# Attention, expert layer and cosine layer on one core: the beginning rebuilt

## The chip, the cores and the metric

The kernel runs on one core of a Trainium2 chip. The metric is the device time of one execution in microseconds. Engines are named as in the profile: PE (matrix multiply; PEld its weight loads), DVE (vector), ACT (scalar), POOL (GpSimd) and SP, which only issues DMAs.

## The reference

A decaying linear attention (batch 4, 8 heads, 768 steps, head width 48) feeds two layers over 3072 tokens of width 384:

```python
for t in range(S):
    cur = einsum('bhd,bhe->bhde', u * kt, vt)
    y[:, :, t] = einsum('bhd,bhde->bhe', rt, state + cur)
    state = w * state + einsum('bhd,bhe->bhde', kt, vt)
x = y in token order, heads side by side            # 3072 x 384
p = domain_probs / (domain_probs.sum(-1) + 1e-9)
out = sum over 4 experts e:  p[:, e] * (relu(x @ w1[e]) @ w2[e])   # inner width 1024
h = out @ w_in                                       # inner width 2048
result = (h * cos(h)) @ w_out
```

## The kernel before

**Layers.** The work on PE is a list of items numbered n. An item is one block of 128 inner columns of a unit (an expert part or a part of the cosine layer) for one tile of tokens: `m_up` multiplies into one of two PSUM tiles `hp` (`ups2[n % 2]`), ACT makes `gh` of it and DVE `gl` (`m_relu`; each float32 value is carried as a high and a low part, three products for one), and `m_down`, two or three items later, multiplies these into three accumulators. A layer block is eight items. The first eight items are plain float32 on 256 tokens, with the raw weight blocks `raw_w` (loaded by `raw_load`) and the raw attention result `x_raw`; from n=8 on the weights come through `w_load` (DMA) and `w_split` (ACT the high part, DVE or POOL the low one), eight tiles ahead of their use.

**Attention.** A cell c is 128 time steps of one batch row in two chunks of 64 (24 cells; the first four are the first time block of each batch row). Within a chunk the sum over steps is a masked product of scores (`a_score_pe`, line 191, then the mask in lines 325 and 330 on DVE) with the values; between chunks a state is carried (`a_state_pe`, line 177). A cell needs, beforehand, its loads (`a_load_tok`, `a_load_t`), `a_kt` and `a_ru` on POOL, `a_r`, `a_rk`, `a_kp` and `a_sum` on DVE. `ONE_AT[c]` is the item in which `a_one(c)` puts the cell's scores, state and the output of cell c-1 on PE; `steps_of` gives the items in which the rest is issued. Cells 4 to 8 stand four items apart, the later ones three.

**The beginning.** The first two cells go ahead of item 0, with steps of their own: `powers` (table of powers of w on DVE), `b_r`, `b_ru`, `b_score`, `b_off`, `b_mask`, `b_in`, `b_y` and `b_x`, which ends in `x_raw`. `tails`, `table` and `table2` make the key table `wk_ch`, which all `a_kp` need; `b_states` makes the first states, and stands with cell 2 at n=2. `warm` keeps PE busy from the start on zeros.

**Order.** Every engine executes its instructions in the order in which the program issues them (`tc.manual_schedule`). What an item issues ahead of its matmuls (raw loads, `w_loads`, `w_splits`, the x splits of n=4 to 6) comes first; `mix` then sets the steps of the item between its matmuls; `later` holds what is to be issued some items on. A wait on ACT or DVE therefore holds whatever was issued behind it. In the code of the first eight items:

```python
if n < BLK - 3: raw_load(n + 3, nc.scalar)
if 2 <= n < BLK:
    w_loads(n - 1)
    w_splits(n - 3, nc.gpsimd if n % 2 else None)
if 4 <= n < 4 + KD: split(xh[0][:, n - 4, ...], xl[0][...], x_raw[:, n - 4, :])
```

Of the kernel before, what the change touches and what calls it, by code (L numbers as in the profile page):

```python
# [7 lines left out]
F32 = mybir.dt.float32  # L8
# [18 lines left out]
def attention_moe_cos_mlp_kernel(  # L27
# [97 lines left out]
    def a_load_t(c):  # L125
        b, i = cells[c]
        t = ld_p.tile([128, 2, HP, 128], F32, tag="rkt", name="rkt", bufs=4)
        (nc.scalar if N_FIRST < c < 6 else nc.sync).dma_start(out=t, in_=rkt[b, i])
        ld.setdefault(c, {})["t"] = t
# [5 lines left out]
    def a_load_tok(c):  # L135
        b, i = cells[c]
        (nc.scalar if N_FIRST < c < 6 else nc.sync).dma_start(out=tok_tile(c).rearrange("q x p d -> q (x p d)"), in_=tok_ch[b, i])
# [5 lines left out]
    def a_r(c):  # L143
        t = ld[c]["t"][:, 0]
        nc.vector.tensor_tensor(out=t, in0=t, in1=pw[:, :, 0:128], op=ALU.mult)
# [9 lines left out]
    def a_rk(c):  # L155
        t = ld[c]["tok"]
        nc.vector.tensor_tensor(out=t[:, 0:2], in0=t[:, 0:2], in1=t[:, 2:4], op=ALU.mult)
# [72 lines left out]
    def b_off(c):  # L230
        so = part_of(2 * c, HP * 4 * C, HP * C).rearrange("q (p t) -> q p t", t=C)
        nc.scalar.activation(out=so, in_=ld[c]["off"].rearrange("q (p t) -> q p t", t=C), func=ACTF.Copy)
        ld[c]["so"] = so

    def b_mask(c):
        s_ = t_p.tile([128, 2, HP, C], F32, tag="s", name="s")
        by = ld[c]["ps"].rearrange("q c (p a t) -> q a c p t", p=HP, a=2)
        wide = [128, 2, HP, C]
        nc.vector.tensor_tensor(out=s_, in0=by[:, 0], in1=mask.unsqueeze(1).unsqueeze(1).to_broadcast(wide), op=ALU.mult)
        nc.vector.copy_predicated(  # L240
            out=s_, mask=eye.bitcast(I32).unsqueeze(1).unsqueeze(1).to_broadcast(wide), data=by[:, 1],
        )
        ld[c]["s"] = s_

    def b_in(c, ps):
        d = ld[c]
        tok, s_, so = d["tok"], d["s"], d["so"]
        d["ps_y"] = ps
        for p in range(HP):
            for ch in range(2):  # L250
                for par in range(2):
                    x0, a0 = 64 * (ch ^ par), 64 * ch
                    nc.tensor.matmul(
                        ps[a0:a0 + 64, par, p * D:p * D + D], s_[x0:x0 + 64, ch, p, :], tok[x0:x0 + 64, 4 + ch, p, :],
                        start=p == 0, stop=ch == 0, skip_group_check=True,
                    )
            for par in range(2):
                x0 = 64 * (1 ^ par)
                nc.tensor.matmul(
                    ps[64:128, par, p * D:p * D + D], so[x0:x0 + 64, p, :], tok[x0:x0 + 64, 3, p, :],  # L260
                    start=False, stop=True, skip_group_check=True,
                )

    def b_y(c):
        yo = t_p.tile([128, DM], F32, tag="yo", name="yo", bufs=2)
        ld[c]["yo"] = yo
        nc.scalar.activation(
            out=yo.rearrange("q (p a d) -> q a p d", a=2, d=D),
            in_=ld[c]["ps_y"].rearrange("q a (p d) -> q a p d", d=D), func=ACTF.Copy,
        )  # L270

    def b_x(c, px):
        for kk in range(KD):
            nc.tensor.transpose(px[:, kk * 128:kk * 128 + 128], ld[c]["yo"][:, kk * 128:kk * 128 + 128], ident)
        nc.scalar.activation(
            out=x_raw[:, :, c * 128:c * 128 + 128], in_=px[:, 0:DM].rearrange("q (k t) -> q k t", k=KD), func=ACTF.Copy
        )

    def b_states():
# [133 lines left out]
    def x_in(i, j, lag, cols=slice(0, TB), step=None):  # L413
        src = acc[j].rearrange("q b d -> q (b d)").rearrange("q (k t) -> q k t", k=KD)
        nc.sync.dma_start(out=src[:, :, cols], in_=yd[i].rearrange("(k q) t -> q k t", k=KD)[:, :, cols])
        x_split(src, j, lag, cols, step or X_STEP)
# [8 lines left out]
    def a_x(c):  # L425
        b, i = cells[c]
        if b == B - 1 and i == 0:
            x_in(0, 0, X0_LAG, slice(256, 512), (0, 0, 0))
        if b == B - 1 and i == 1:
            x_in(1, 1, XT_LAG)  # L430
        ld.pop(c)

    NC_ = len(cells)
# [7 lines left out]

    on_pe = (a_one,)
    ONE_AT = {c: 4 * c - 6 for c in range(N_FIRST, 9)}
    ONE_AT.update({c: 29 + 3 * (c - 9) for c in range(9, NC_ + 1)})
    BEGIN = {3: ((a_load_tok, 0), (a_load_t, 0), (a_ru, 1)), 4: ((a_load_tok, 3), (a_load_t, 4), (a_ru, 5)), 5: ((a_load_tok, 6), (a_load_t, 7), (a_ru, 8))}

    def steps_of(c):
        at, p = ONE_AT[c], ONE_AT[c - 1]
        wide = at - p > 3
        two = ONE_AT.get(c - 2, 0)  # L450
        yield from BEGIN.get(c, ((a_load_tok, two - 1), (a_load_t, two), (a_ru, p - (2 if wide else 1))))
        yield from ((a_kt, p), (a_r, p + wide), (a_rk, p + 2), (a_kp, p + 2), (a_sum, p + 2 + wide))

    steps = {}
    for c in range(N_FIRST, NC_ + 1):
# [40 lines left out]
    def raw_load(q, eng=None):  # L496
        (eng or nc.sync).dma_start(out=raw_w[0, 0, q], in_=moe_wb[q])
# [219 lines left out]
    x2_tile = {}  # L717
    x2d = {}

    wu_a = const.tile([128, 128], mybir.dt.bfloat16, name="wu_a")  # L720
    wu_b = const.tile([128, 512], mybir.dt.bfloat16, name="wu_b")

    def warm(n):
        if n == 0:
# [53 lines left out]
            double(n)  # L778
            n *= 2

    def tails():
        for a in range(2):
            x = slice(64 * a, 64 * a + 64)
            for ch in range(2):
                last = 2 * C - 1 - C * (ch ^ a)
                nc.scalar.activation(out=tk[x, :, ch], in_=pw[x, :, last:last - C if last >= C else None:-1], func=ACTF.Copy)

    def table():
        pt = ps_d.tile([128, TB], F32, tag="up", name="pt").rearrange("q (p a e) -> q a p e", p=HP, a=2)
        for p in range(HP):  # L790
            nc.tensor.transpose(pt[:, :, p, :], tk[:, p].rearrange("q c t -> q (c t)"), ident)
        return pt

    def table2(pt, a):
        x = slice(64 * a, 64 * a + 64)
        nc.scalar.activation(out=wk_ch[x], in_=pt[x, ::-1 if a else 1, :, 0:D], func=ACTF.Copy)
# [8 lines left out]
    def prob_load():  # L805
        nc.sync.dma_start(out=p_in, in_=moe_domain_probs.rearrange("(p t) e -> p t e", t=32))
# [48 lines left out]
    N_DEC = N_ATT + 4  # L855
    X_STEP = (0, 0, 1)
    X_LAG = 1
    XT_LAG = 2
    TAIL = 2
    Y_LAG = 1  # L860
    WARM_FIRST = 17
    X0_LAG = 2

    def on_pe_call(f):
# [18 lines left out]

    with tc.manual_schedule():
        nc.vector.memset(wu_a, 0.0)
        nc.scalar.activation(out=uw1, in_=wu_a[:, 0:2 * HP].bitcast(F32), func=ACTF.Copy)
        nc.vector.memset(wu_b, 0.0)
        setup()
        warm(WARM_FIRST)
        powers()  # L890
        raw_load(0)
        a_load_tok(2)
        a_load_t(2)
        nc.sync.dma_start(out=uu_ch.rearrange("q a p d -> q (a p d)"), in_=u_ch)
        for c in range(N_FIRST):
            b_load(c, 3, 5, 1)
        raw_load(1)
        prob_load()
        raw_load(2)
        for c in range(N_FIRST):  # L900
            b_r(c)
            a_kt(c, nc.vector)
        nc.vector.tensor_tensor(out=w128, in0=pw[:, :, 2 * C:2 * C + 1], in1=pw[:, :, 2 * C:2 * C + 1], op=ALU.mult)
        for c in range(N_FIRST):
            b_ru(c)
        off = x_bank()
        b_score(0, pair_ps, off[:, 0:HP * C])
        b_off(0)
        tails()
        b_mask(0)  # L910
        b_score(1, dense_ps[0], off[:, HP * C:2 * HP * C])
        b_off(1)
        b_mask(1)
        a_ru(2)
        a_kt(2)
        b_in(0, dense_ps[1][:, :, 0:HD])
        b_y(0)
        pt = table()
        table2(pt, 0)
        table2(pt, 1)  # L920
        b_in(1, pair_ps[:, :, 0:HD])
        b_y(1)
        b_x(0, dense_ps[0][:, 0])
        b_x(1, dense_ps[0][:, 1])
        a_r(2)
        a_rk(2)
        a_sum(2)
        for c in range(N_FIRST + 1):
            a_kp(c)
        ps_d_ctx.close()  # L930
        ps_u = ctx.enter_context(tc.tile_pool(name="ps_u", bufs=1, space=bass.MemoryType.PSUM))
        ups2 += [ps_u.tile([128, TB], F32, name=f"hp{x}") for x in range(2)]
        for hp in ups2:
            nc.tensor.matmul(hp[:, 256:512], wu_a, wu_b[:, 0:256], start=True, stop=True)
        ps_a = ctx.enter_context(tc.tile_pool(name="ps_a", bufs=1, space=bass.MemoryType.PSUM))
        downs = []
        pend = []
# [1 line left out]
        for n in range(NI + 4):  # L939
            live = n < NI  # L940
            moe2 = False
            if n < BLK - 3:
                raw_load(n + 3, nc.scalar)
            if 2 <= n < BLK:
                w_loads(n - 1)
                w_splits(n - 3, nc.gpsimd if n % 2 else None)
            if n == 3:
                prob_norm()
                prob_scale()
                prob_store()  # L950
# [287 lines left out]
```

## Time and profile before

| | |
|---|---|
| median of 3 runs | 1261.89 us (1261.34 to 1262.25) |
| profiled execution | 1262.03 us, its span 1260.3 us |
| PE busy | 1246.5 us, 99% of the span |
| DVE, ACT, POOL busy | 773.0, 492.9, 193.6 us |
| DMA | 126.53 MB, mean 100 GB/s |

The span is from the first to the last instruction of the program; the rest of the execution's time lies around it. In the timeline a row is a run of like instructions: start, duration, engine, line, operation, out<-in, count, and in brackets the idle time before it with what ended it. "q" behind an engine is its sequencer, which issues DMAs.

### The profile page before, as it was taken

The page shows a single profiled execution, that of the slowest core. Times are in us where ns is not written, and L with a number is a line of the kernel's source. Part 1 is how long each engine was busy: PE and PEld are TensorE (multiplying, and loading weights), DVE is VectorE, ACT ScalarE, POOL GpSimd, SP SyncE. Part 2 cuts the span into 40 slices and gives each one's busy share as a digit, 9 for nine tenths or more (in the row PEclk, how much of TensorE's full clock was granted, in tenths as well). Part 3 has the DMA queues.
Part 4 walks back from the last instruction along what each step waited for, and adds up shares of the span by engine and source line. Part 5 has one row for each costly group of instructions (what it writes and reads, how often), then busy time and mean ns, then how long its engine had stood idle before and what let it go on. Part 6 is the DMA issues. An engine that isn't in the chain of part 4 may idle for free.

```text
span 1260.3 us, 20498 instructions
## 1 busy us (share of the span) xinstructions
PE 1246.5 (99%) x8453; PEld 1038.8 (82%) x8453; DVE 773.0 (61%) x1259; ACT 492.9 (39%) x879; POOL 193.6 (15%) x190
## 2 busy tenths in 40 slices
PE   9999999999999999999999999999999999999997
PEld 7898888788888888888888888888888888888886
DVE  6897747766264464546645543326776777777665
ACT  4442313223221131112111222216777677767774
POOL 3664323421100000111111111112000100010100
PEclk9999999999999999999999999999999999999999
DMA  8635634444242243223331410123001400160601
GB/s 322 220 117 177 196 125 154 124 137 111 84 139 59 84 134 109 67 76 127 107 92 52 133 43 9 59 78 122 1 1 42 160 26 25 36 203 13 196 11 47
DMA packets 72501, 126.53 MB, mean 100 GB/s; under 512 B 23153, under 2 KB 44754, under 8 KB 72402
## 3 DMA queue, kind: packets, MB, share of 16 engines
q1 hardware_dynamic: 65634, 93.38, 23.6%
q0 software_dynamic: 4608, 25.17, 6.4%
q10 hardware_dynamic: 2160, 6.62, 1.5%
q8 instruction: 67, 1.10, 0.4%
q14 instruction: 32, 0.26, 0.1%
HBM read 101.90 MB, written 23.25 MB: 99 GB/s over the span
## 4 chain that ended last, share of the span: by engine, by line


## 5 line engine op out<-in xcount | busy, mean ns | idle before, releaser
L595 PE MATMUL hp<-xh,w 128*128 128x512 f32 (+1 forms) x888 | 341.3, 384 | 1.6 <-DVE gl L609 1.6
L596 PE MATMUL hp<-xl,w 128*128 128x512 f32 (+1 forms) x888 | 338.1, 381 | 0.5 <-DVE xl L118 0.5
L597 PE MATMUL hp<-xh,w 128*128 128x512 f32 (+1 forms) x888 | 337.9, 380 | 0.2 <-issue 0.2
L670 PE MATMUL a<-gh,w 128*128 128x512 f32 (+1 forms) x880 | 335.0, 381 | 0.0
L671 PE MATMUL a<-gh,w 128*128 128x512 f32 (+1 forms) x880 | 334.8, 380 | 0.0
L672 PE MATMUL a<-gl,w 128*128 128x512 f32 (+1 forms) x880 | 334.7, 380 | 0.0
L608 ACT ACTIVATE gh<-hp 128x512 fp32r<-128x512 f32 (+1 forms) x200 | 114.5, 573 | 539.7 <-PE hp L597 532.6
L609 DVE SCALAR_TENSOR_TENSOR gl<-hp,gh 128x512 fp32r<-128x512 f32 (+1 forms) x200 | 131.1, 657 | 299.5 <-ACT gh L608 298.8
L595 PEld LDWEIGHTS hp<-xh,w 128*128 128x128 f32 x888 | 166.9, 188 | 35.7 <-DVE gl L609 2.9
L597 PEld LDWEIGHTS hp<-xh,w 128*128 128x128 f32 x888 | 166.9, 188 | 32.1
L596 PEld LDWEIGHTS hp<-xl,w 128*128 128x128 f32 x888 | 167.0, 188 | 31.9 <-DVE xl L118 0.7
L670 PEld LDWEIGHTS a<-gh,w 128*128 128x128 f32 x880 | 165.5, 188 | 32.0 <-ACT rr L626 0.4
L672 PEld LDWEIGHTS a<-gl,w 128*128 128x128 f32 x880 | 165.5, 188 | 31.7
L671 PEld LDWEIGHTS a<-gh,w 128*128 128x128 f32 x880 | 165.5, 188 | 31.5
L693 POOL TENSOR_TENSOR acc<-acc,pm 128x512 f32<-128x512 f32 (+1 forms) x57 | 72.5, 1302 | 537.9 <-DVE pm L692 537.9
L628 DVE SCALAR_TENSOR_TENSOR hs<-rr,hs 128x512 f32<-128x512 f32 x96 | 67.4, 702 | 62.8 <-ACT rr L627 62.8
L626 ACT ACTIVATE rr<-rr 128x512 f32<-128x512 f32 x96 | 60.8, 633 | 86.4 <-DVE rr L621 86.4
L620 DVE SCALAR_TENSOR_TENSOR rr<-ni,hs 128x512 f32<-128x512 int32 x96 | 66.3, 691 | 45.6 <-ACT ni L619 45.6
L621 DVE SCALAR_TENSOR_TENSOR rr<-ni,rr 128x512 f32<-128x512 int32 x96 | 66.5, 692 | 3.3
L507 POOL DMA_DIRECT2D w<-dec_all x32 | 17.1, 535 | 333.0 <-PE a L672 332.1
L118 DVE TENSOR_TENSOR gl<-hs,gh 128x512 fp32r<-128x512 f32 x96 | 66.0, 688 | 0.7 <-ACT gh L117 0.7
L618 ACT ACTIVATE hs<-hp 128x512 f32<-128x512 f32 x96 | 57.2, 596 | 17.8 <-PE hp L597 17.6
(151 smaller groups left out, 1066.2 us busy)
## 6 DMA issues: line engine op xcount, KB each, us to landing
w<-dec_all POOLq DMA_DIRECT2D x32, 768.0 KB, 4.6
s<-in_moe_wb_dram SPq DMA_DIRECT2D x53, 384.0 KB, 4.0
draw<-in_moe_wb_dram SPq DMA_DIRECT2D x32, 384.0 KB, 4.3
dec_all<-dout SPq DMA_DIRECT2D x32, 384.0 KB, 3.0
tok<-in_tok_ch_dram SPq DMA_DIRECT2D x19, 576.0 KB, 5.4
rkt<-in_rkt_dram SPq DMA_DIRECT2D x21, 512.0 KB, 3.8
pb<-pn SPq DMA_DIRECT2D x24, 256.0 KB, 5.0
out_dram<-acc SPq DMA_DIRECT2D x17, 256.0 KB, 2.5
```

Source lines behind the costliest of these rows:

```text
L595: nc.tensor.matmul(hp, wh[:, kk, :], x_h[:, kk, :], start=kk == 0, stop=False)
L596: nc.tensor.matmul(hp, wh[:, kk, :], x_l[:, kk, :], start=False, stop=False)
L597: nc.tensor.matmul(hp, wl[:, kk, :], x_h[:, kk, :], start=False, stop=kk == KD - 1)
L608: nc.scalar.activation(out=gh, in_=hp, func=ACTF.Relu)
L609: nc.vector.scalar_tensor_tensor(out=gl, in0=hp, scalar=0.0, in1=gh.bitcast(F32), op0=ALU.max, op1=ALU.subtract)
L620: nc.vector.scalar_tensor_tensor(out=rr, in0=ni, scalar=-PI2_HI, in1=hs, op0=ALU.mult, op1=ALU.add)
L621: nc.vector.scalar_tensor_tensor(out=rr, in0=ni, scalar=-PI2_LO, in1=rr, op0=ALU.mult, op1=ALU.add)
L628: nc.vector.scalar_tensor_tensor(out=hs, in0=rr, scalar=1.0, in1=hs, op0=ALU.subtract, op1=ALU.mult)
L670: nc.tensor.matmul(a, wh[:, ds], gh, start=q == 0, stop=False)
L671: nc.tensor.matmul(a, wl[:, ds], gh, start=False, stop=False)
L672: nc.tensor.matmul(a, wh[:, ds], gl, start=False, stop=q == BLK - 1)
L693: nc.gpsimd.tensor_tensor(out=o, in0=o, in1=m, op=ALU.add)
```

## The change

Warming uses three float32 matmuls on zeros in `acc` where 17 bf16 ones stood. The masks and the products with the values of the first two cells go in halves of two heads (`h`), `b_y` and the transposes in parts; the copy into `x_raw` moves from ACT to DVE. `tails` is split, its first half ahead of `b_ru`; `b_off` of both cells comes behind both scores. The key table and the three `a_kp` move to n=1, `b_states` and cell 2 from n=2 to n=3. Loads on SP are reordered, and one more raw block is on SP; the raw and staged weight loads on ACT, and cell 3's loads, come an item later; the splits stay. The two dummy matmuls that filled the upper half of `hp` become two copies on ACT. `a_rk` comes an item earlier for cells three items apart, `a_kp` an item later for cells four items apart; the x splits of the first two token tiles are spread.

```diff
-    def b_mask(c):
+    def b_mask(c, h):
+        if h == 0:
+            ld[c]["s"] = t_p.tile([128, HP, 2, C], F32, tag="s", name="s")
+        heads = slice(2 * h, 2 * h + 2)
...
-    def b_in(c, ps):
+    def b_in(c, ps, h):
...
-        for p in range(HP):
+        for p in range(2 * h, 2 * h + 2):
...
-    def b_x(c, px):
-        for kk in range(KD):
+    def b_x(c, px, k0, k1):
+        for kk in range(k0, k1):
             nc.tensor.transpose(px[:, kk * 128:kk * 128 + 128], ld[c]["yo"][:, kk * 128:kk * 128 + 128], ident)
-        nc.scalar.activation(
-            out=x_raw[:, :, c * 128:c * 128 + 128], in_=px[:, 0:DM].rearrange("q (k t) -> q k t", k=KD), func=ACTF.Copy
+
+    def b_xc(c, px, k0, k1):
+        nc.vector.tensor_copy(
+            out=x_raw[:, k0:k1, c * 128:c * 128 + 128],
+            in_=px[:, k0 * 128:k1 * 128].rearrange("q (k t) -> q k t", t=128),
         )
...
-            x_in(0, 0, X0_LAG, slice(256, 512), (0, 0, 0))
+            x_in(0, 0, X0_LAG, slice(256, 512), (0, 0, 1))
         if b == B - 1 and i == 1:
-            x_in(1, 1, XT_LAG)
+            x_in(1, 1, XT_LAG, step=(0, 1, 2))
...
     ONE_AT = {c: 4 * c - 6 for c in range(N_FIRST, 9)}
+    ONE_AT[N_FIRST] = 3
...
-    BEGIN = {3: ((a_load_tok, 0), (a_load_t, 0), (a_ru, 1)), ...
+    BEGIN = {3: ((a_load_tok, 1), (a_load_t, 1), (a_ru, 2)), ...
...
-        yield from ((a_kt, p), (a_r, p + wide), (a_rk, p + 2), (a_kp, p + 2), (a_sum, p + 2 + wide))
+        yield from ((a_kt, p), (a_r, p + wide), (a_rk, p + 1 + wide), (a_kp, p + 2 + wide), (a_sum, p + 2 + wide))
...
-    wu_a = const.tile([128, 128], mybir.dt.bfloat16, name="wu_a")
-    wu_b = const.tile([128, 512], mybir.dt.bfloat16, name="wu_b")
+    wu_a = part_of(0, 1280, 128)
+    wu_b = part_of(1, 512, 512)
...
-        pt = ps_d.tile([128, TB], F32, tag="up", name="pt").rearrange("q (p a e) -> q a p e", p=HP, a=2)
+        pt = x_bank().rearrange("q (p a e) -> q a p e", p=HP, a=2)
...
-    XT_LAG = 2
+    XT_LAG = 1
-    WARM_FIRST = 17
+    WARM_FIRST = 3
...
         raw_load(0)
-        a_load_tok(2)
-        a_load_t(2)
-        nc.sync.dma_start(out=uu_ch.rearrange("q a p d -> q (a p d)"), in_=u_ch)
         for c in range(N_FIRST):
             b_load(c, 3, 5, 1)
         raw_load(1)
+        a_load_t(2)
+        raw_load(2)
+        a_load_tok(2)
+        nc.sync.dma_start(out=uu_ch.rearrange("q a p d -> q (a p d)"), in_=u_ch)
+        raw_load(3)
         prob_load()
-        raw_load(2)
...
+        tails(0)
         for c in range(N_FIRST):
             b_ru(c)
         off = x_bank()
         b_score(0, pair_ps, off[:, 0:HP * C])
-        b_off(0)
-        tails()
-        b_mask(0)
         b_score(1, dense_ps[0], off[:, HP * C:2 * HP * C])
-        b_off(1)
-        b_mask(1)
+        for c in range(N_FIRST):
+            b_off(c)
+        tails(1)
+        for c in range(N_FIRST):
+            for h in range(2):
+                b_mask(c, h)
         a_ru(2)
         a_kt(2)
-        b_in(0, dense_ps[1][:, :, 0:HD])
-        b_y(0)
-        pt = table()
-        table2(pt, 0)
-        table2(pt, 1)
-        b_in(1, pair_ps[:, :, 0:HD])
-        b_y(1)
-        b_x(0, dense_ps[0][:, 0])
-        b_x(1, dense_ps[0][:, 1])
+        b_in(0, dense_ps[1][:, :, 0:HD], 0)
+        b_in(0, dense_ps[1][:, :, 0:HD], 1)
+        b_y(0, 0, HP)
+        b_in(1, pair_ps[:, :, 0:HD], 0)
+        b_y(1, 0, 2)
+        px = (x_bank(), dense_ps[1][:, 0])
+        b_x(0, px[0], 0, KD)
+        b_xc(0, px[0], 0, KD)
+        b_in(1, pair_ps[:, :, 0:HD], 1)
+        b_x(1, px[1], 0, 1)
+        b_xc(1, px[1], 0, 1)
+        b_y(1, 2, HP)
+        b_x(1, px[1], 1, KD)
+        b_xc(1, px[1], 1, KD)
         a_r(2)
...
-        for c in range(N_FIRST + 1):
-            a_kp(c)
...
-        for hp in ups2:
-            nc.tensor.matmul(hp[:, 256:512], wu_a, wu_b[:, 0:256], start=True, stop=True)
...
-            if n < BLK - 3:
-                raw_load(n + 3, nc.scalar)
-            if 2 <= n < BLK:
-                w_loads(n - 1)
+            if n < 2:
+                nc.scalar.activation(out=ups2[1 - n][:, 256:512], in_=wu_b[:, 0:256], func=ACTF.Copy)
+            if 2 <= n < BLK - 2:
+                raw_load(n + 2, nc.scalar)
+            if 3 <= n < BLK:
+                w_loads(n - 2)
                 w_splits(n - 3, nc.gpsimd if n % 2 else None)
-            if n == 3:
+            if n == 1:
+                pt = table()
+                for a in range(2):
+                    table2(pt, a)
+                for c in range(N_FIRST + 1):
+                    a_kp(c)
+            if n == 4:
                 prob_norm()
```

## Rows read from the trace of the kernel before

**Rows 1.** Stages: stretch, length, engines' busy (count), PE clock, DMA share, GB/s.

```profile
15.17:37.19 22.02, 22.02 (x327) 19.18 (x325) 15.74 (x27) 9.59 (x22) 10.43 (x11) 1.00 0.90 308
37.19:110.00 72.81, 69.99 (x1314) 66.72 (x1313) 62.78 (x97) 26.98 (x62) 44.92 (x36) 1.00 0.56 180
```

**Rows 2.** PE's waits from 18 to 110 us: total, times, longest.

```profile
PE hp L595 <- DVE gl L609: 1.4, 2, 1.1
PE hp L357 <- DVE gl L609: 0.7, 1, 0.7
PE hp L596 <- DVE xl L118: 0.5, 1, 0.5
```

**Rows 3.** PE's waits from 150 to 400 us.

```profile
PE pair_ps L177 <- DVE kp L166: 0.9, 1, 0.9
PE hp L357 <- DVE gl L609: 0.4, 1, 0.4
```

**Rows 4.** Timeline of the beginning: start, duration, engine, line, operation, count, idle before.

```profile
1.34 5.80 PE L728 MATMUL hp<-wu_b,wu_a 128*128 128x512 bf16 x17 [1.34 <-DVE wu_b L887]
...
5.14 0.15 PEld L728 LDWEIGHTS <-wu_a 128*128 128x128 bf16 x1 [0.27 <-issue]
...
5.47 1.18 PEld L728 LDWEIGHTS <-wu_a 128*128 128x128 bf16 x6 [0.18 <-issue]
...
6.07 2.45 ACT L206 ACTIVATE acc<-acc,uw 128x128 f32<-128x128 f32 x8 [3.74 <-DVE acc L199]
...
8.97 1.44 ACT L786 ACTIVATE acc<-pw 64x256 f32<-64x256 f32 x4
...
9.36 0.63 PE L225 MATMUL px<-acc,rkt 64*64 64x64 f32 x16
...
10.98 0.66 PE L791 MATMUL pt<-ident,acc 128*128 128x128 f32 x4
11.10 0.49 ACT L267 ACTIVATE yo<-dy_ps 128x384 f32<-128x384 f32 x1 [0.27 <-PE dy_ps L259]
...
12.65 0.55 PE L274 MATMUL ds_ps<-ident,yo 128*128 128x128 f32 x3
...
15.17 2.75 PE L589 MATMUL hp<-acc,raw_xh 128*128 128x256 f32 x12
```

**Rows 5.** What line 325 waited for in the whole run: total us, times.

```profile
  PE pair_ps L177: 21.1, 14
```

**Rows 6.** Timeline of ACT and its DMA issues, 14 to 28 us.

```profile
14.84 0.44 ACTq L137 DMA_DIRECT2D tok<-in_tok_ch_dram  x1
...
22.64 0.44 ACTq L137 DMA_DIRECT2D tok<-in_tok_ch_dram  x1
...
27.77 0.84 ACT L504 ACTIVATE w<-s 128x768 fp32r<-128x768 f32 x1 [0.89 <-DMA s<-in_moe_wb_dram]
```

**Rows 7.** DMA issue at 22.64 us: KB, us from issue to landing.

```profile
tok<-in_tok_ch_dram ACTq DMA_DIRECT2D x1, 576.0 KB, 6.5
```

**Rows 8.** Timeline of DVE, POOL and PE, 27.5 to 33 us.

```profile
27.62 0.55 DVE L166 TENSOR_TENSOR kp<-tok,wk_ch 128x384 f32<-128x384 f32 x1
28.96 1.83 DVE L118 TENSOR_TENSOR xl<-acc,xh 128x256 fp32r<-128x256 f32 x1 [0.80 <-ACT xh L117]
...
30.46 1.19 POOL L153 TENSOR_TENSOR tok<-tok,uu_ch 128x384 f32<-128x384 f32 x1
...
31.16 0.54 PE L177 MATMUL pair_ps<-tok,kp 64*48 64x48 f32 x32
```

**Rows 9.** Timeline of DVE, 50 to 55 us.

```profile
51.56 2.19 DVE L166 TENSOR_TENSOR kp<-tok,wk_ch 128x384 f32<-128x384 f32 x1
53.67 0.41 DVE L609 SCALAR_TENSOR_TENSOR gl<-hp,gh 128x256 fp32r<-128x256 f32 x1
```

**Rows 10.** Timeline of DVE, 58 to 63 us.

```profile
59.47 2.58 DVE L118 TENSOR_TENSOR xl<-acc,xh 128x256 fp32r<-128x256 f32 x2
```

**Rows 11.** Timeline of DVE, 231 to 239 us.

```profile
233.40 1.64 DVE L157 TENSOR_TENSOR tok<-tok 128x384 f32<-128x384 f32 x1
```

## The prediction: what the rebuilt beginning does to the time

> **What bounds the kernel now.** I read the busy shares by stage first, then what PE waited for, then the timeline of the beginning. Layer work starts at 15.17 us. From there to 37.19 PE is busy without a break (22.02 of 22.02) while the DMA engines stand at 0.90; from 37.19 to 110 PE misses 2.8 us (69.99 of 72.81), with DVE busy for 62.78 [rows 1]. So a gain can only come from a layer stream that starts earlier, or from the few waits of PE after that. These are, from 18 to 110 us, 1.4 and 0.7 us for gl and 0.5 for xl [rows 2], later 0.9 us for kp and 0.4 for gl [rows 3]: about 4 us in all. What stands at 0.90 of its capacity when the stream begins is the DMA, and this decides whether an earlier start is kept.
>
> **The change, part by part.** Numbers n are layer blocks (items), c attention cells; score(0) is b_score of cell 0.
>
> *Warming.* The 17 bf16 matmuls of 128x512 begin at 1.34. The weight load at 5.14 stands 0.42 us (0.15 busy, 0.27 idle) from the one before; from 5.47 six fit into 1.18 us [rows 4]. 512 columns in 0.42 us is the 1.2 GHz level, in 0.2 us the 2.4 GHz one: PE had run back to back for about 4.1 us when the clock rose, and the warming ends near 7.0. The new warming is 3 float32 matmuls. Six of 128x256 (12 records of line 589) take the 2.6 us from 15.17 [rows 4], 0.43 each at the high level; 128x512 is 0.86 there and 1.72 at the low one, three are 2.6 to 5.2 us. Their memsets are twice as wide, so they start at about 1.7 and, with a rise after the same 4.1 us, end near 6.2. Score(0) then goes with the scaled parts that ACT makes, 0.3 us apart from 6.07 (eight in 2.45), the fourth done at 7.35 [rows 4], and not behind the warming: 0.3 us earlier.
>
> *Off blocks and tails.* The first two tails move into ACT's empty time before 6.07: free. But b_off(0) now stands behind both scores, whose off products share one PSUM bank. A reader is ordered here behind all writers of its bank: line 325 reads the score columns and waits for line 177, which writes other columns of that bank [rows 5]. The off products of cell 1 ended at 9.99 (9.36 + 0.63 [rows 4]), now at 9.7; b_off(0) starts at 9.75, b_off(1) at 10.05, and the two late tails (0.36 each, four in 1.44) end at 11.15. Then b_y(0) starts at 11.15, where it started at 11.10 [rows 4]: the 0.3 us is spent. The halved masks cost 0.41 us a piece by the 128x256 operation of line 609 [rows 9], eight of them 3.3; they begin with score(0)'s end near 8.0 and end by 11.3, and no step waits for them longer than for off.
>
> *Values in halves, copies on DVE, table gone.* With 0.49 for b_y [rows 4] as the price of each 384-wide copy, 0.33 for half of one, 0.55 for three transposes (line 274 [rows 4]): yo(0) 11.65, its transposes 12.25; cell 1's first half of b_y 12.0, second half of b_in 12.6, of b_y 13.0, transposes 13.55, DVE copy (0.41) 14.0. The first k-slice of n=0 needs only cell 1's first copy and starts at 13.4, the others at 14.05; n=0's up part ends at 14.9, where it ended at 16.46 (15.17 and three times 0.43): minus 1.5. The four table transposes (0.66 us with the drain [rows 4], 0.45 in a stream) come in at n=1: plus 0.45. So n=2 and n=3 are 1.1 us early. The three kp wait for a_rk(2) and this for uu_ch, now behind two more weight blocks; by about 20.2 they are done, and the states, at n=3 now, want them between 19.7 and 21: 0 to 0.6, I take 0.
>
> *Loads.* On ACT, cell 3's loads move from n=0 (14.84 [rows 6]) to behind the table copies at n=1, about 16.4: 1.55 us later, less the raw block (393 KB, 1.28 us at the 308 GB/s of rows 1) that SP now brings. The staged weight blocks are issued an item later (n=3, 4, 5), their splits stay at n=4, 5, 6: one item of 2.6 us from issue to use, not two. The second of them (w1) is split on ACT, in order, and that began at 27.77, after 0.89 us of waiting for it [rows 6]. Cell 4's tok (576 KB) is now ahead of it in the queue; before, it was issued at 22.64 and landed 6.5 us later, 1.35 us after w1 [rows 6, 7]. So w1 comes 1.35 + 0.3 = 1.65 us later, at 29.4. Bounds: 0 (the DMA catches up in its idle tenth) to 2.5 (the raw block no relief).
>
> *What waits for w1.* ACT's split of w1, then its xh, then on DVE xl, at 28.96 for 1.83 us [rows 8]. Kp(3) ran before all this, at 27.62 in 0.55 us. With the states at n=3 the distance to n=6 is three items, "wide" is false for cell 3, and kp(3) falls into n=5, in order behind xl. Xl ended 3.0 us after w1 landed; with 0.5 for kp: 32.9. State(3) on PE (line 177), at 31.16 before [rows 8], would be due at 29.6 and starts at 32.95: PE waits 3.3 us, the lead of 1.1 is lost and 1.8 more. The visit and the rest of n=6 queue behind it. Bounds: kp in time, minus 1.1; w1 at its late bound and kp slowed by POOL, plus 3.5. I take plus 1.8.
>
> Here a rule of the Trainium skill speaks against the change. The page "SBUF — State Buffer", section "Who interferes with whom", says that a DVE instruction with two SBUF inputs and a GpSimd instruction that reads SBUF keep each other out for a whole instruction. The rows agree: kp took 0.55 us at 27.62 and 2.19 at 51.56 [rows 8, 9]. By it kp(3) would stand behind a_ru(4) too (30.46, 1.19 long), and the total be some 0.7 higher.
>
> *Later steps, each by the wait that it touches.* (a) Kp of cells 4 to 8 an item later. At 51.56 it ran 2.19 us ahead of gl, which came at 53.67 [rows 9] and cost PE the longest wait of 1.1 [rows 2]. Now gl goes first; kp, 1.4 us beside POOL, then ends some 0.65 after state(5) wants it: minus 0.5. At the other wait for gl (0.3, and 0.1 for refilling): minus 0.4. (b) Second half of block 0's split: the third slice goes behind a_r(6). It was the second of two that took 2.58 us from 59.47 [rows 10], and PE waited 0.5 for it already; with POOL free by then 0.45 more. (c) Block 1's splits over three items: they wait for a DMA that is issued at the same item, and DVE has the same sum behind it: 0. (d) A_rk of cells 9 and later an item earlier: at 233.40 it stood 1.64 us ahead of kp [rows 11], and PE waited 0.9 + 0.4 [rows 3]; both go, with 0.1 for refilling: minus 1.4.
>
> **Sum.** 1.8 - 0.5 - 0.4 + 0.45 - 1.4 = -0.05. The profiled execution took 1262.03 (span 1260.3, 1.7 around it), 0.14 above the median of the runs, 1261.89; forecast 1261.8.
>
> **Rivals.**
>
> *The lead is kept.* If ACT's later loads find the DMA emptier, w1 lands early enough for kp(3) to end before 29.6. For it: the DMA is at 0.90, not 1, up to 37.19. Against: ACT waits for these loads already, with two items of distance. Then -1.1 - 0.5 - 0.4 + 0.45 - 1.4 = -2.95: 1258.9. Chance 0.21.
>
> *Kp late at every visit*, on the other side. Cells 4 to 8 now make kp in the item just ahead of its use, beside POOL's subtractions and a_ru. It decides from the point where kp ends later than some 0.9 us into the visit's item (the first third of its up products and the scores go ahead of the state). The price of a visit is 0 to 1.64 (2.19 less 0.55), half taken, 0.8; four visits, since (a) counts the fifth: 3.2, and (a)'s 0.9 not had: -0.05 + 4.1, 1265.9. For it: DVE is at 0.86 of that stage. Against: most of these kp had no POOL beside them in the item they move to. Chance 0.13.
>
> *The warming falls short*: the change does not do what it says. If the clock rises only after the three matmuls, scores, values and transposes run at the low level; they are some 3.5 us of PE's chain, so plus 0 to 3.5, half taken: 1263.5. It decides from a warming that ends before the rise; the margin is 0.5 us. Chance 0.09. The Trainium skill's page "TensorE: Matmul & The Clock Gate", section "What's actually happening", calls the warm-up a budget of time and not of matmuls, and one that varies from run to run; by that, some executions would show this rival. The one rise in this trace cannot tell.
>
> **How the numbers follow.** The forecast has 0.57 (its own range 1260.0 to 1263.7, by the bounds of w1 and of (a) and (b)). What can be told from no change is 0.2%, 2.5 us: 1259.4 to 1264.4. Faster: 0.18 of the first rival and 0.05 of the forecast's edge, 0.23. Slower: 0.12 of the second, 0.02 of the third, 0.03 of the forecast, 0.17. Same: 0.60. Range 1258.5 to 1265.3: outside are part of the first rival below and most of the second above.
>
> **What would show it.** Right: line 589 first at 13.2 to 13.8; PE idle between 29 and 33 us until kp (line 177); ACT's split of the second staged block at 28.5 to 30; state(3) at 32 to 34; no wait near 236. Wrong: no idle time of PE between 25 and 37 (the first rival); waits for kp at several visits from 43 to 90 (the second); score records at twice their pitch, and no faster warming before 6.5 (the third). A first line 589 later than 14.5 breaks the working of the start.

## The result, and the profile after

The changed kernel took 1269.54 us (median of 6 runs, 1267.39 to 1269.77), the kernel before in the same rounds 1262.54 us (6 runs, 1261.34 to 1263.3). The ratio is 1.0053, 95% interval 1.004 to 1.0066: slower, and above the range that was given (1258.5 to 1265.3). The profiled execution took 1269.72 us with a span of 1267.7, where before it was 1262.03 and 1260.3. In the later rounds, those of the experiments, the kernel before had medians of 1262.6 to 1262.9 with 23 of its 78 runs at 1265 to 1268.5; the ratios given there take all of these in, so most of them lie lower than the ratio of the medians. In the code of the layers a line of before stands 7 or 8 lines further down now: line 589 is 597, line 504 is 512, line 609 is 617, line 357 is 364.

Stages of the changed kernel first, with the columns of [rows 1]; the cuts are the first layer matmul, item 6 and item 7, and the last row takes out the stretch at the low clock.

```profile
15.32:30.71 15.39, 15.39 (x192) 13.33 (x193) 10.61 (x19) 5.55 (x14) 6.90 (x8) 1.00 0.73 251
30.71:42.33 11.62, 7.76 (x126) 6.42 (x125) 8.84 (x12) 4.97 (x11) 5.34 (x5) 0.71 0.58 203
42.33:110.00 67.67, 64.37 (x1156) 61.63 (x1155) 54.23 (x85) 24.54 (x56) 38.50 (x33) 1.00 0.55 175
...
35.84:41.83 5.99, 5.99 (x88) 5.21 (x89) 5.16 (x8) 3.05 (x8) 1.91 (x3) 0.50 0.29 77
```

One item holds nearly all of it. Item 6 took 11.62 us; before, it went from 30.12 to 34.78, 4.66 us. PE was busy for 7.76 of the 11.62 and idle for 3.86, and its clock was 0.71 in the mean. The last row says when: from the end of the idle time to 41.83 the granted clock was 0.50, that is 1.2 and not 2.4 GHz. So the 6.96 us that the item lost are 3.86 of waiting and 3.1 of the same work at half the clock.

What PE waited for from 15 to 130 us; before, there was no wait for kp in this stretch [rows 2].

```profile
PE pair_ps L177 <- DVE kp L166: 5.3, 2, 3.9
PE hp L603 <- DVE gl L617: 1.4, 2, 0.8
PE hp L604 <- DVE xl L118: 1.0, 1, 1.0
PE hp L597 <- DVE acc L281: 0.5, 1, 0.5
```

The timeline of ACT, DVE, POOL and PE around the long wait, which answers to [rows 6, 8]:

```profile
25.00 0.33 ACT L319 ACTIVATE se<-pair_ps 128x192 f32<-128x192 f32 x1 [1.92 <-DVE s L332]
...
25.87 1.02 ACTq L501 DMA_DIRECT2D s<-in_moe_wb_dram  x1
...
31.52 0.84 ACT L512 ACTIVATE w<-s 128x768 fp32r<-128x768 f32 x1 [3.16 <-DMA s<-in_moe_wb_dram]
...
32.70 1.82 DVE L118 TENSOR_TENSOR xl<-acc,xh 128x256 fp32r<-128x256 f32 x1 [1.45 <-ACT xh L117]
34.20 1.18 POOL L153 TENSOR_TENSOR tok<-tok,uu_ch 128x384 f32<-128x384 f32 x1
34.45 1.34 DVE L166 TENSOR_TENSOR kp<-tok,wk_ch 128x384 f32<-128x384 f32 x1
...
35.84 0.89 PE L177 MATMUL pair_ps<-tok,kp 64*48 64x48 f32 x32 [3.86 <-DVE kp L166]
```

And the issue of the same block in the kernel before:

```profile
22.16 0.45 ACTq L493 DMA_DIRECT2D s<-in_moe_wb_dram  x1
```

Read the timeline downwards: the second staged block is issued at 25.87 and ACT waits for it until 31.52; xh, xl and kp follow one another, and the state of cell 3 comes last. The transfer itself took no longer: the block landed 5.6 us after its issue, as in the kernel before (issued at 22.16, split at 27.77 [rows 6]). It was the issue that came 3.71 us later: one item later, in a stream that was itself 0.59 late, and behind cell 2's step on ACT (line 319), which the move to n=3 puts just ahead of it and which waited until 25.00 for the mask. It is the chain that the prediction drew, with each link some 2 to 3 us later. Kp took 1.34 us beside POOL's subtraction, 0.55 alone [rows 8].

The beginning, with the columns of [rows 4]:

```profile
1.68 5.49 PE L736 MATMUL hp<-acc,acc 128*128 128x512 f32 x6 [1.68 <-DVE acc L895]
...
10.32 0.66 ACT L232 ACTIVATE acc<-px 128x256 f32<-128x256 f32 x2 [1.51 <-PE px L225]
...
11.82 0.49 ACT L271 ACTIVATE yo<-dy_ps 128x384 f32<-128x384 f32 x1
...
13.96 0.29 DVE L281 COPY acc<-dy_ps 128x128 f32<-128x128 f32 x1 [0.31 <-PE dy_ps L278]
...
14.39 0.41 PE L278 MATMUL dy_ps<-ident,yo 128*128 128x128 f32 x2 [0.54 <-DVE acc L281]
14.84 0.42 DVE L281 COPY acc<-dy_ps 128x256 f32<-128x256 f32 x1 [0.59 <-PE dy_ps L278]
...
15.32 1.56 PE L597 MATMUL hp<-acc,raw_xh 128*128 128x256 f32 x6 [0.52 <-DVE acc L281]
```

The layers start at 15.32 us, 0.15 later than before, not at 13.4. The three float32 matmuls fill 5.49 us and run at the low clock throughout; by the trace's clock records the rise came at 7.70 us, where it came at 5.37 before.

Last the wait at 96.8 us, where cell 8's kp runs beside POOL and takes 2.15 us:

```profile
94.50 1.83 POOL L513 TENSOR_TENSOR w<-raw_xl,w 128x768 fp32r<-128x768 f32 x1 [0.65 <-ACT w L512]
94.59 2.15 DVE L166 TENSOR_TENSOR kp<-tok,wk_ch 128x384 f32<-128x384 f32 x1
...
96.80 0.57 PE L177 MATMUL pair_ps<-tok,kp 64*48 64x48 f32 x32 [1.47 <-DVE kp L166]
```

Following the start of each item against the same item before gives the account of the whole run: +0.59 up to item 6, +6.96 in it, then -1.33 (54 us) and +0.40, +0.47 (69 us, the split of block 0), -0.46 (87 us), +1.44 (96.8), +0.73 in block 1 (0.77 and 0.93, less 0.97 that before lost there), -1.26 (236 us): +7.54, and the spans differ by 7.4.

The 0.77 stands at item 29, and the order on DVE shows where it comes from. The step `a_rk` of cell 9 (line 157), an item earlier now, stands ahead of the gl that PE waits for; before, it stood behind it. First the changed kernel, then the one before:

```profile
103.87 1.37 DVE L157 TENSOR_TENSOR tok<-tok 128x384 f32<-128x384 f32 x1
105.16 0.41 DVE L617 SCALAR_TENSOR_TENSOR gl<-hp,gh 128x256 fp32r<-128x256 f32 x1
...
105.62 0.38 PE L603 MATMUL hp<-xh,w 128*128 128x256 f32 x1 [0.61 <-DVE gl L617]
```

```profile
95.47 0.41 DVE L609 SCALAR_TENSOR_TENSOR gl<-hp,gh 128x256 fp32r<-128x256 f32 x1
95.80 1.03 DVE L157 TENSOR_TENSOR tok<-tok 128x384 f32<-128x384 f32 x1
```

This is read from the order; no run puts that one step back alone, and in the kernel before with two good parts (below) the same order cost 0.11.

### The profile page after: what moved, and what is told of

It reads as the page before. It is cut to its first block, busy times and chain, and to the rows that moved or that the text cites. A ratio compares the mean times of both kernels' runs of the same rounds, so it can differ in the third digit from the quotient of the medians.

```text
span 1267.7 us, 20497 instructions
## 1 busy us (share of the span) xinstructions
PE 1249.2 (99%) x8440; PEld 1040.6 (82%) x8440; DVE 778.2 (61%) x1266; ACT 492.4 (39%) x880; POOL 191.4 (15%) x190
## 4 chain that ended last, share of the span: by engine, by line
```

## The experiments

Theory: the staged weight blocks, issued one item later, are late for ACT's split; x split and kp stand behind it in order, PE idles, and the idle time brings the clock down as well. Rivals: kp's own place is the fault; the low clock costs nothing; the layer's later steps are the loss; the rebuilt beginning is. The changed kernel was not run again in these rounds: a difference against it is one between medians of different rounds, in which those of the kernel before differ by up to 0.35 us.

**Kp of cell 3 alone, an item earlier.**

```diff
-        yield from (... (a_kp, p + 2 + wide), ...)
+        yield from (... (a_kp, 4 if c == 3 else p + 2 + wide), ...)
```

> The changed kernel with one step moved: the key product kp of cell 3 (line 166) is issued by VectorE at item n=4, ahead of the x split of that item, and not at n=5 behind it. Theory (the wait of the state matmul of cell 3, 3.86 us, is the loss, with the fall of the granted clock that follows it, about 3 us more): no wait of line 177 near 32 us, the granted clock stays at 1.0 from 35 to 42 us, and the time falls by about 6.9 us, to some 1262.6. Rival (ScalarE's split of the third staged weight block, which waited for its DMA until 35.34, is next in line and holds item 7 until about 37): part of the wait stays, item 7 starts near 37 and not near 35.4, the time falls by about 5.2 us, to some 1264.3. Rival (the x split is late for itself, and kp ahead of it only makes it later): the time is unchanged or higher.

Measured: 1268.94 us (10 runs), ratio 1.0036 [1.0021, 1.005]. Neither figure came. The wait at 32 us is gone, as expected: item 7 starts at 36.65 and not at 42.33, 5.7 us earlier; that is nearer to the rival's 37 than to the theory's 35.4, and a wait of 0.58 us for ACT's gh stays in that item. But four items on, the next late weight block makes the same chain with cell 4. In this timeline ACT waits 4.73 us for the block, kp stands behind the block's low half on DVE, and PE waits 2.87; the window row behind it shows the low clock again, 3.41 us of it.

```profile
45.73 0.84 ACT L512 ACTIVATE w<-s 128x768 fp32r<-128x768 f32 x1 [4.73 <-DMA s<-in_moe_wb_dram]
...
46.60 0.96 DVE L513 TENSOR_TENSOR w<-s,w 128x768 fp32r<-128x768 f32 x1 [5.15 <-ACT w L512]
47.48 0.55 DVE L166 TENSOR_TENSOR kp<-tok,wk_ch 128x384 f32<-128x384 f32 x1
...
48.08 0.57 PE L177 MATMUL pair_ps<-tok,kp 64*48 64x48 f32 x32 [2.87 <-DVE kp L166]
```

```profile
48.70:52.11 3.41, 3.29 (x53) 3.09 (x53) 1.73 (x5) 1.15 (x2) 1.81 (x1) 0.50 0.65 255
```

So kp's place is only where the lateness comes out. A wait taken away by reordering is moved while the transfers behind it are late.

**PE kept at work during the wait.**

```diff
         a_score_pe(c, pair_ps, HD, True)
+        if c == 3:
+            fill = x_bank()
+            for _ in range(4):
+                nc.tensor.matmul(fill, wu_a, wu_b, start=True, stop=True)
```

> The changed kernel with four matmuls added that no result uses (float32, 128x512, zeros) on TensorE between score(3) and the state of cell 3, that is in the stretch in which it waits. Theory (idling makes the clock fall, and the low clock from 35.0 to 41.8 us costs about 3 us by itself): the state matmul still starts near 35.8, the clock stays at 1.0, and the time falls by about 3.0 us, to some 1266.5. Rival (the low clock costs nothing, because the items that run in it wait for splits and gelus anyway): the time stays at 1269.5 within 0.6. Rival (the fall of the clock has nothing to do with the idle time): the clock falls all the same, time unchanged.

Measured: 1268.25 us (10 runs, 1266.29 to 1270.46), ratio 1.0032 [1.0017, 1.0047]: 1.3 below the changed kernel, not 3.0. The trace of one execution (1266.29) is clear, though. The windows are the fill and the stretch after it:

```profile
31.27:35.18 3.91, 3.70 (x15) 1.44 (x9) 3.16 (x3) 2.09 (x5) 2.94 (x2) 1.00 0.85 322
35.18:42.00 6.82, 6.82 (x107) 6.17 (x108) 5.11 (x8) 2.84 (x8) 3.62 (x4) 1.00 0.52 157
```

The clock stays at 1.00, and from the state of cell 3 (35.18) to item 7 (38.84) it takes 3.66 us, where the changed kernel took 6.49 (35.84 to 42.33): 2.83 us for the low clock in that place, near the 3.0 expected. Why the median gains less than half of it stays open. A fall elsewhere is one way: the mean clock of the ten runs was 0.997 to 0.999, and the experiments show falls in other places too; no trace of these other runs was taken.

**Staged weight blocks loaded one item earlier, as before.**

```diff
+            if 2 <= n < BLK:
+                w_loads(n - 1)
             if 3 <= n < BLK:
-                w_loads(n - 2)
                 w_splits(n - 3, ...)
```

> The changed kernel with the DMAs of the staged weight blocks issued one item earlier, from n=2, as in the kernel before; their splits stay where they are. Theory (the wait of cell 3's state is at its root the late second staged weight block: ScalarE waited 3.16 us for it at 31.52, and the x split and kp queue behind that): the wait of line 177 falls from 3.86 to 1 us or less, the clock stays at 1.0, and the time falls by 6 to 7 us, to 1262.6 to 1263.6. Rival (the transfers are bound by the DMA engines, busy 0.73 of that stretch, so that an earlier issue lands hardly earlier and holds up the tok loads): the wait falls by less than 1.5 us, the time to some 1266 to 1268.

Measured: 1264.62 us (10 runs), 4.9 below the changed kernel; ratio 0.9995 [0.998, 1.001], the same as before and clear of the changed kernel's [1.004, 1.0066]; by the medians it is 1.7 above before. The timeline shows the second block issued at 20.44 and ACT waiting 0.49 us for it; PE's wait is 0.33.

```profile
20.44 0.47 ACTq L501 DMA_DIRECT2D s<-in_moe_wb_dram  x1
...
28.35 0.84 ACT L512 ACTIVATE w<-s 128x768 fp32r<-128x768 f32 x1 [0.49 <-DMA s<-in_moe_wb_dram]
...
32.91 0.57 PE L177 MATMUL pair_ps<-tok,kp 64*48 64x48 f32 x32 [0.33 <-DVE kp L166]
```

The theory holds for the wait and the clock at 35 us. Its figure was 1 us too low: in the trace the wait for cell 8's kp (1.48 us) now brought a fall of the clock as well, so that 2.74 us were lost there and not 1.44. The window behind that wait:

```profile
93.09:96.50 3.41, 3.41 (x18) 3.41 (x18) 3.28 (x7) 2.08 (x5) 1.95 (x3) 0.50 0.23 47
```

**The late loads alone, in the kernel before.**

```diff
-            if 2 <= n < BLK:
-                w_loads(n - 1)
+            if 3 <= n < BLK:
+                w_loads(n - 2)
+            if 2 <= n < BLK:
```

> The kernel before with one part of the change alone: the DMAs of the staged weight blocks are issued one item later, from n=3; their splits stay. Theory (this one edit is the loss: the load of a block and its split are then one item apart, which is less than the transfer takes, ScalarE waits, and the x split and kp queue behind it): the state of cell 3 waits 3 to 4.5 us for kp near 32 us, the granted clock falls behind it, and the time rises by 5 to 8 us, to 1267.5 to 1270.5. Rival (it takes the rest of the change too, the other order of raw blocks and tok loads ahead of them): ScalarE waits less than 1.5 us, TensorE hardly, the time rises by less than 1.5 us.

Measured: 1267.52 us (8 runs) beside 1262.61, ratio 1.0033 [1.0016, 1.005]: plus 4.9, the same size as the gain of the reverse edit, just below the 5 to 8 expected. The place was another. Cell 3's kp runs in time here (its state was not moved), and PE waits where ACT's and DVE's next steps are held by the block:

```profile
30.89 0.84 ACT L504 ACTIVATE w<-s 128x768 fp32r<-128x768 f32 x1 [3.09 <-DMA s<-in_moe_wb_dram]
...
32.36 0.25 PE L357 MATMUL hp<-s,tok 64*48 64x64 f32 x1 [0.84 <-ACT gh L604]
...
44.81 0.84 ACT L504 ACTIVATE w<-s 128x768 fp32r<-128x768 f32 x1 [4.91 <-DMA s<-in_moe_wb_dram]
...
47.50 0.25 PE L357 MATMUL hp<-s,tok 64*48 64x64 f32 x1 [2.92 <-DVE gl L609]
```

```profile
49.20:52.61 3.41, 3.41 (x18) 3.41 (x17) 2.96 (x6) 1.63 (x5) 1.76 (x3) 0.50 0.29 100
```

One edit, 4.9 us in either direction: the late loads cost PE time in both kernels, and in the changed one they are the main cause. That the two figures are equal is chance, since the waits stand at different places.

**The layer's later steps put back.**

```diff
-        yield from (... (a_kp, p + 2 + wide), ...)
+        yield from (... (a_kp, p + 2 + (c == 5)), ...)
-x_in(0, 0, X0_LAG, slice(256, 512), (0, 0, 1))
+x_in(0, 0, X0_LAG, slice(256, 512), (0, 0, 0))
-x_in(1, 1, XT_LAG, step=(0, 1, 2))        # XT_LAG = 1
+x_in(1, 1, XT_LAG)                         # XT_LAG = 2
```

> The changed kernel with the layer's steps behind 42 us put back: kp of cells 4 and 6 to 8 one item earlier (cell 5 stays late), and the x splits of blocks 0 and 1 with the steps and the lag of the kernel before. Theory (these moves cause the waits of 1.47 us at 96.8 for kp of cell 8, of 0.6 and 0.8 us at 105.6 and 115.2 for the gelu of block 1, and 0.96 at 69.2 for the split of block 0): minus 1.44, minus 1.70, minus 0.47, and the waits that the kernel before had there come back, plus 0.97 and plus 0.46, so about minus 2.2, to some 1267.4. Rival (the waits come from the layers' running 7 us later against the cells' transfers): they stay, the time is unchanged within 0.6.

Measured: 1266.98 us (10 runs), ratio 1.0015 [1.0001, 1.003]: minus 2.6 against the changed kernel, where 2.2 was expected. In its waits the one of cell 8 and half of block 0's are gone; the 3.9 us of cell 3 stand, and in this execution a raw weight block was late for PE itself:

```profile
PE pair_ps L177 <- DVE kp L166: 3.9, 1, 3.9
PE hp L597 <- DMA raw_xl<-in_moe_wb_dram: 1.7, 1, 1.7
PE hp L603 <- DVE gl L617: 1.1, 3, 0.6
```

The agreement is in part luck. By the starts of the items, the changed kernel loses 1.27 us against the one before from item 7 to item 36, and this one gains 0.09: 1.4 us come from the moved steps, not 2.2. In block 1 nothing came of the 0.73 expected (minus 1.70, plus 0.97); the wait of 0.62 at item 29 stays (104.4 us here).

**Two good parts alone, in the kernel before.**

```diff
-        yield from (... (a_rk, p + 2), (a_kp, p + 2), ...)
+        yield from (... (a_rk, p + 1 + wide), (a_kp, p + 2 + (c == 5)), ...)
```

> The kernel before with two parts of the change alone: kp of cell 5 one item later, so that it no longer stands ahead of the gelu's low half at 54 us, and the rk step of the cells from 9 on one item earlier. Theory (both are gains that the changed kernel keeps under its losses): the wait of 1.3 us near 54 us and that near 236 us go, nothing else moves, minus 2.6 us, to some 1260.3 beside 1262.9 for the kernel before. Rival (what goes there comes back at the next cell, since VectorE has the same work in the same stretch): the offset that the trace shows behind 60 us or behind 260 us is 0 again, the time is unchanged within 0.6.

Measured: 1260.59 us (12 runs), ratio 0.9987 [0.997, 1.0004]; 2.0 below the medians of before, by an interval that just takes in no change. In the trace the starts of the items show each part: -1.33 at 54 us, of which 0.41 comes back at 58 and 0.32 at 92, and -1.27 at 236 us, which is kept; at 400 us 1.9 are left of the 2.6. The rival holds for a quarter. After [rows 2], the 1.4 and 0.7 us of gl are now 0.3 and 0.5; after [rows 3], the 0.9 of kp is gone.

**Cell 1's transposes in the x bank.**

```diff
-px = (x_bank(), dense_ps[1][:, 0])
+x1 = x_bank()
+px = (x1, x1)
```

> The changed kernel with the transposes of cell 1 in the x bank as well, so that nothing of the pool that the layer's hp banks take over is read by VectorE's last copies. Theory (the first layer matmul waits for the release of that whole pool, that is for the last copy of line 281 ending at 15.26, and not for its own first k-slice): the first layer matmul starts before the last copy has ended, 0.3 to 0.5 us earlier, the end of item 0's up 0.0 to 0.4 us earlier. Rival (it waits for its own operand): it still starts behind the last copy.

Measured (one execution): 1269.91 us. The timeline shows line 597 at 14.16, before the last copy, and its second slice waiting for that copy:

```profile
14.16 1.81 PE L597 MATMUL hp<-acc,raw_xh 128*128 128x256 f32 x6
14.36 0.42 DVE L281 COPY acc<-px 128x256 f32<-128x256 f32 x1 [0.59 <-PE px L278]
14.84 0.73 PEld L597 LDWEIGHTS hp<-acc,raw_xh 128*128 128x128 f32 x4 [0.48 <-DVE acc L281]
...
21.67 0.25 PE L177 MATMUL px<-tok,kp 64*48 64x48 f32 x2 [0.44 <-DVE kp L166]
```

So the first layer matmul had waited for banks that the last copy still read, and not for its own slice; whether for the old pool as a whole or for one bank of it, this run does not tell (with a clock that rose at nearly the same time, 6.54 for 6.40, it stood at 14.82 in the experiment on the later steps). In this execution the lead is not kept: the first states, at n=3, wait 0.44 us for a kp that ran beside POOL, and item 4 waited 0.9 for a raw block.

**The old warming in the changed kernel.**

```diff
-wu_a = part_of(0, 1280, 128)
-wu_b = part_of(1, 512, 512)
+wu_a = const.tile([128, 128], mybir.dt.bfloat16, name="wu_a")
+wu_b = const.tile([128, 512], mybir.dt.bfloat16, name="wu_b")
-WARM_FIRST = 3
+WARM_FIRST = 17
```

> The changed kernel with the warming of the kernel before (17 bf16 matmuls in place of 3 float32 ones). Theory (the granted clock rises late after the float32 warming, at 7.70 us in the changed kernel and 5.37 us before, and the key score of cell 0 starts late for it): the clock rises near 5.4, the score starts near 6.6 and not 7.1, the first layer matmul at 14.6 to 14.9, and the time falls by 0.4 to 0.6 us, to some 1269.0. Rival (the beginning is bound by VectorE's and ScalarE's chain and by the loads, not by TensorE's clock): the score starts earlier, the first layer matmul within 0.1 us of 15.32, the time unchanged.

Measured: 1269.09 us (7 runs), ratio 1.0048 [1.0032, 1.0065]; 0.45 lower, too little to tell. Here the clock rose at 6.13, the warming lasted to 7.52, and the score started no earlier:

```profile
1.34 6.18 PE L736 MATMUL hp<-wu_b,wu_a 128*128 128x512 bf16 x17 [1.34 <-DVE wu_b L895]
...
7.45 1.10 PE L216 MATMUL pair_ps<-acc,rkt 64*64 64x128 f32 x32
...
15.40 1.56 PE L597 MATMUL hp<-acc,raw_xh 128*128 128x256 f32 x6 [0.52 <-DVE acc L281]
```

The score starting at 7.45 fits neither theory; that line 597 stays within 0.1 of 15.32 fits the rival. With the float32 warming the clock rose at 7.70, 6.54, 5.58 and 4.92 us in four kernels with this same beginning, and the first layer matmul stood at 15.32, 14.82, 14.72 and 14.70. With this warming an earlier rise goes with an earlier first layer matmul, by up to 0.6 us; with the bf16 one, in its one trace here, a rise at 6.13 brought nothing, since the warming itself lasted longer (7.52 for 7.17).

**Loads and later steps both corrected.** The edits of the third and the fifth experiment together.

> The changed kernel with both corrections together: staged weight blocks loaded one item earlier, and kp of cells 4 and 6 to 8 and the x splits of blocks 0 and 1 as in the kernel before. Theory (late weight blocks, late kp at cell 8 with the fall of the clock behind it, and the splits are the whole loss): 1264.6 (loads alone), minus 2.7 for cell 8, minus 0.5 and 0.7 for the splits, plus 0.5 that comes back at 87 us and 0.2 elsewhere: some 1261.3, that is a ratio to the kernel before of 0.998 to 1.000. Rival (the rebuilt beginning itself costs, by its later first layer matmul and by its x bank): at least 1263.5, not faster than the kernel before.

Measured: 1261.76 us (12 runs, 1260.79 to 1263.08), ratio 0.9986 [0.9974, 0.9998]. As expected, and the rival falls: the rebuilt beginning is not slower. It beats both kernels, the one before by 0.14% (0.9 us by the medians), which is less than matters. PE's waits from 15 to 130 us are down to these and two more of 0.5:

```profile
PE hp L603 <- DVE gl L617: 0.9, 2, 0.6
PE hp L597 <- DMA raw_xl<-in_moe_wb_dram: 0.8, 1, 0.8
PE hp L597 <- DVE acc L281: 0.5, 1, 0.5
```

**The rest of the loads too.** On top of that, raw blocks an item earlier and kp of cell 3 at n=4.

```diff
-            if 2 <= n < BLK - 2:
-                raw_load(n + 2, nc.scalar)
+            if 1 <= n < BLK - 3:
+                raw_load(n + 3, nc.scalar)
-        yield from (... (a_kp, p + 2 + (c == 5)), ...)
+        yield from (... (a_kp, 4 if c == 3 else p + 2 + (c == 5)), ...)
```

> The corrected version (staged weight blocks one item earlier, kp of cells 4 and 6 to 8 and the x splits as before) with two more steps put back: the raw blocks from the fifth on loaded one item earlier, from n=1, and kp of cell 3 issued at n=4. Theory (what is left of the loss between 28 and 36 us is the raw block that item 4 waited for, 0.79 us, and the 0.3 us of kp): both go, 1261.8 minus 1.0, some 1260.7, a ratio to the kernel before of 0.998. Rival (the transfers have no room: a raw block loaded earlier pushes the staged block back): the wait moves to the state of cell 3 or to item 7, the time stays at 1261.8 or rises by up to 4 us.

Measured: 1261.89 us (12 runs), ratio 0.9989 [0.9977, 1.0001]: no gain in time, which is the rival's figure. In the trace PE waits for nothing between 15 and 50 us, so the theory holds there, and the rival's moved wait did not come; items 4 to 11 start 0.03 us earlier than in the kernel before, though the first layer matmul stands 0.47 earlier. The difference is about the size of the 0.45 that the sum gave the key table at n=1. Beside the two good parts alone (1260.59) it is not better. The rebuilt beginning, with its loads in time, is worth nothing that these runs can tell.

## Why the prediction was wrong

The forecast was 1261.8, the profiled execution took 1269.72, 7.9 more. By the steps of the prediction:

- **The start: failed.** Its own mark was a line 589 later than 14.5; it came at 15.32. The sum had item 2 or 3 early by 1.1, it was late by 0.59: 1.7 us. Three links were too short. First, the warming was to end at 6.2 with a rise on the way; it ended at 7.17, all at the low clock, which is the third rival's mechanism, and the scores that follow came late: b_off(0) at 10.32 (9.75 said), b_y(0) at 11.82 (11.15). In three of the eight traces with this warming it ended before the rise, where 0.09 was given; in the other five the rise came at 4.92 to 6.69 and b_off(0) at 9.70 to 9.88, so this link is worth some 0.6 us. Second, b_y(0) to the end of the last copy took 3.44 us, not 2.85: the second half of cell 1's products ran from 12.91 to 13.59 where the sum had 0.35, and the last two transposes waited for the copy of the first slice, which reads their bank (13.96 + 0.29; PE from 14.39). Third, the first matmul waited for the last copy, since that copy still read the pool that its banks were taken over from; the step "needs only cell 1's first copy" is shown wrong for these banks by the x bank experiment. It also shows an earlier start being lost again at n=3.
- **W1 and the state of cell 3: mechanism right, size wrong.** That the block comes late, that xl and kp stand behind it in order, and that PE waits at line 177, all held. The split stood at 31.52 for 29.4: the term had 1.65 us for the place in the queue, while the transfer was as long as before and its issue 3.71 later. The wait was 3.86 for 3.3 (by the sum's own lead of 1.1 the state was due at 30.06 and not at 29.6, which makes it 2.9). What the term left out is the clock: the idle time was priced as idle time alone, and 3.1 us more followed it (2.83 by the fill experiment). From 1.1 early to 1.8 late was 2.9 us; the item lost 6.96. This is the 4.1 us that carried the time out of the range, 1.0 for the longer wait and 3.1 for the clock: even its late bound, plus 3.5, had no clock in it.
- **The rule on DVE and POOL** (the Trainium skill, "SBUF — State Buffer", "Who interferes with whom") was put beside the sum as plus 0.7. Kp at 1.34 us beside POOL where it takes 0.55 alone agrees with it, and is 0.8.
- **(a)** The two gains came (-1.33 less 0.40, for -0.5; -0.46 for -0.4), but cell 8's kp, put where POOL subtracts for 1.83 us, cost 1.44. That is the second rival at one visit of the four that it named: 0.95 worse in sum.
- **(b)** 0.47 for 0.45. **(c)** 0.73 for 0, but not by the splits. With the splits put back, in three kernels, item 29 lost the same 0.78 (0.77 in the changed kernel), and what comes and goes behind it sums to -0.01 to -0.40 there, to -0.04 in the changed kernel. By the order on DVE the 0.77 belongs to the earlier `a_rk` of cell 9, a price of (d) that the sum did not have. **(d)** -1.26 for -1.4.
- The sum of these differences: 1.7 + 4.1 + 0.95 + 0.73 + 0.14 = 7.6; the other 0.3 lie around the span (2.0 us for 1.7).

The first rival (the lead is kept) fell. What the prediction had not asked is what its own 3.3 us of idle PE would do to PE afterwards.

## What to carry to other kernels

An item of work between a load and its use is only worth what it lasts: here 2.6 us stood against a transfer that took 5.6, and moving the issue one item later cost 4.9 us in two different kernels, each time at a place that depended on what stood in line behind the wait. Price an idle stretch of PE of a few microseconds at its length and once more at the work that follows at the lower clock. When a wait is removed by moving its consumer, look for the next consumer of the same late transfer before counting the gain.

## What the runs showed of the hardware

- With a wait of 3.86 us PE stood at 1.2 GHz for 6.8 us (35.0 to 41.8, the fall before the wait's end); with 3.89 and 4.22 (later steps put back, x bank) it did the same. With 4.54 (old warming), 2.87 and 2.92 it stood there for 3.4, the fall after the wait's end. After waits of 1.46 and 1.48 at cell 8 it fell for 3.4 us in two kernels; after 1.46 to 1.48 in four others (changed kernel, fill, x bank, old warming) it did not. The same idle time can have either outcome.
- The rise at the beginning is as loose: 4.92 to 7.76 us with the float32 warming in the eight traces that have it, 4.83 to 6.13 with the bf16 one in four. The Trainium skill ("TensorE: Matmul & The Clock Gate", "What's actually happening") says that the warm-up varies from run to run, and puts the variation of its end at ±500 ns. These traces agree that it varies, but by more: 2.84 us among the eight.
